# Attention followed by spectral mixing on one core: four weight products moved into the attention loop, the fill work spread evenly, and three first sums placed in PSUM ahead of z

## The chip, the core and the metric

The kernel runs on one core of a Trainium2 chip. The core has TensorE (PE, matrix products into the PSUM memory), VectorE (DVE), ScalarE (ACT), GpSimd (POOL) and SyncE (SP). Each engine executes its own instructions in order, and semaphores tie the engines to one another. Sixteen DMA engines move data; here POOL issues the loads of weights and inputs, and SP issues the stores. The metric is the device time of one execution in microseconds (us); less is better.

## What is computed

```python
phi(x) = [exp(x@w_phi - m), exp(-(x@w_phi) - m)]      # m = max |x@w_phi| of the row
x = num / den          # q_p (k_p^T v) / (q_p sum k_p), 8 batches x 8 heads x 576 x 64
X = rfft(x, axis=1)    # x as 8 x 576 x 512; the first 64 modes are kept
Yr = Xr@w_r - Xi@w_i   # w_r, w_i: 64 modes x 512 x 512, float32
Yi = Xr@w_i + Xi@w_r
y = irfft(Y, n=576)
u = x + y
out = u + relu(u @ w_ch)
```

The weights `w_r` and `w_i` are 134 MB of the 164 MB that the core reads. They go through the DMA engines once and are turned into bf16 on the way. The kernel never forms `u`: it keeps `x` and `x @ w_ch`, and adds the inverse transform of the modes `y` to the first and of `z = y @ w_ch` to the second.

## The kernel before

**Attention loop** (lines 503 to 572). Sixteen units `(g, bp)` (four groups of 128 channels by four pairs of batches) run through a software pipeline, `n` from -2 to 16. In step `n` the loop handles four units at once: `P` (unit n-1: forward transform, `freq` and `keep_x`), `Q` (unit n: attention), `K` (n+1) and `R` (n+2). `keep_x` writes the modes of unit P into `XTb[g % 2]`, so groups 0 and 2 share a buffer, and 1 and 3. Step 16 has only `P`.

**Weight products.** There are 64 of them; each takes one 1 MB block (8 modes x 128 channels, real or imaginary part). I number them 0 to 63 in the order of `order`. Products 0 to 15 belong to group 0, 16 to 31 to group 1, 32 to 43 to group 2, 44 to 55 to group 3; the last eight are groups 2 and 3 of modes 48 to 63. `mix` issues eight matmuls of 32 rows each. The odd product of a pair completes a block `o` of eight modes. `some(n)` in the loop issues the next `n` products, and `next_w(1)` after each asks POOL for the next weight block that has no buffer yet; a block's buffer is free once its product is done. PE executes a product in its place in the program, so a product whose weights have not landed holds up everything behind it on PE. `X` (line 505) sets how many products a step carries: 8 in step 4, 3 in each later one, none in step 16. 40 products are issued in the loop and 24 after it.

**After the loop** (lines 573 to 973). One `while` loop takes the remaining products from `mixq`. `left` is how many are still to come after the one just issued. Between the products it works off `todo`, a list of 76 items, `fill(n)` at a time:

- `turn` of the first of 36 chunks (128 tokens x 512 channels), and 36 `hold(i)`: each turns the next chunk with PE transposes, multiplies chunk `i` by `w_ch` (four matmuls) and copies the result to `xw`. For the last three chunks the result stays in PSUM instead. The first nine `hold` also carry the steps of `inverse_tables()`, which are mostly DVE work. In all 37 items.
- 39 absorb items: `only_x` and `only_w` for the last three chunks (six items), `all` for the other 33. An absorb adds the inverse transform of the modes in `yall` to the chunk's `x` (`keep_x`, DVE) and that of `zall` to its `xw` (`keep_w`, ACT). These need blocks 0 to 5, the eight chunks of batches 0 and 1 that come last need block 6 too.

With group 3 the odd product completes a block: `yst` (DVE), four transposes, `yT`, the product with `w_ch` and `zst` follow, and `put` sends `yst` and `zst` to `yall` and `zall` by DMA. Block 5 is complete with product 55 (`left` = 8), block 6 with 59, block 7 with 63. The pace of `fill` is set by lines 925 to 929.

**PSUM** has two pools in this part: `pst`, four single banks (tile `pt`, function `bank`), and `pst2`, two pairs of banks (tile `pp`, function `banks`). An absorb with an even number takes a pair and one with an odd number two single banks. The tile framework makes an instruction wait for a free buffer and orders accesses of different engines to one tile.

**The last stage** (lines 908 to 999). `seq` lists 20 outputs (`Last`): two single chunks `(0,0)` and `(0,1)`, then pairs of chunks, two of them of "ninth rows" (`n == 8`), and two single chunks at the end. For each, `base(1)` and `base(0)` put `xw` and `x` into PSUM (q and p), `straight` or `late` add the last blocks' modes (`zst`/`yst`, or `yl`), `relu` takes q through ACT into `rl`, and `store` adds p on DVE and sends the result off. Outputs whose p needs no `base(0)` (the stored chunks and ninth rows, `later`) have `x` added by POOL instead. `ahead` says whose q is made while an output's p is made. `seq[0].base(1)`, `seq[0].base(0)` stand before product 63, `seq[1].base(1)` right behind it.

Of the kernel before, what the change touches and what calls it, by code (L numbers as in the profile page):

```python
# [10 lines left out]
F32 = mybir.dt.float32  # L11
# [8 lines left out]
DMODEL = 512  # L20
# [23 lines left out]
def kernel(  # L44
# [14 lines left out]
    pe, dve, act = (InOrder(tc, e) for e in (nc.tensor, nc.vector, nc.scalar))  # L59
# [297 lines left out]
    mixq = []  # L357
# [45 lines left out]
    def sc(i):  # L403
# [4 lines left out]
        out=ang[:, :, 1, :],  # L408
        in0=sf.unsqueeze(2).to_broadcast([128, 5, 64]),
        in1=mf.unsqueeze(1).to_broadcast([128, 5, 64]),  # L410
# [5 lines left out]
        out=rnd, in0=ang, scalar1=1.0 / S_, scalar2=MAGIC, op0=ALU.mult, op1=ALU.add)  # L416
# [71 lines left out]
    def some(n):  # L488
        for _ in range(n):
            if mixq:  # L490
                key = mixq.pop(0)
                mix(*key, wts.pop(key), XTb[key[0] % 2], lambda: one([128, DMODEL]))
                if key not in held:
                    next_w(1)
# [7 lines left out]

    for n in range(-2, len(units) + 1):
        P, Q, K, R = (unit(n + i) for i in (-1, 0, 1, 2))
        X = 0 if n < 4 or not Q else 6 if n == 4 else 3
        if Q:
            Q.exp_q(0)
        if K:
            K.rows_k(0)
            K.exp_k(0)  # L510
        if Q:
            Q.weigh_v2()
            if unit(n + 2):
                unit(n + 2).load_v()
        if P:
            P.freq()
            P.keep_x()
            if P.bp == NP - 1:
                mixq += [key for key in order if key[0] == P.g and (P.g < 2 or key[1] < 12)]
        if Q:  # L520
            Q.cols_q(1)
            Q.exp_q(1)
        some(1 if X else 0)
        if K:
            K.rows_k(1)
            K.exp_k(1)
        if Q:
            Q.kv()
        some(2 if n == 4 else 0)
        if K:  # L530
            K.rows_q(0)
            K.rows_k(2)
            K.rows_q(2)
            K.rows_q(1)
        if Q:
            Q.cols_q(2)
            Q.keep_kv()
            Q.exp_q(2)
        if K:
            K.exp_k(2)  # L540
            K.weigh_v()
        some(1 if X else 0)
        if R:
            R.turn_k(0)
        if K:
            K.shift_q()
        if R:
            R.turn_k(1)
        if Q:
            Q.num(0)  # L550
        if K:
            K.cols_q(0)
        if R and unit(n + 4):
            unit(n + 4).load_k()
        if Q:
            Q.num(6)
        if R:
            R.turn_q(0)
            R.turn_q(1)
            if unit(n + 4):  # L560
                unit(n + 4).load_q()
        if Q:
            Q.num(12)
        some(X - 2)
        if n == -1:
            forward_table()
        if n < 3:
            next_w((2, 3, 2, 3, 2)[n + 2])
        elif n == 3:
            next_w(1)  # L570
        if n == 6:
            pool.dma_start(wchb, moe_w_ch.rearrange("(dc p) e -> p dc e", p=128))
# [8 lines left out]
    def bank(shape=(128, DMODEL), dt=F32):  # L581
        return pst.tile(list(shape), dt, name="pt", tag="pt")

    def banks(dt=F32):
        return pst2.tile([128, 2, DMODEL * (1 if dt == F32 else 2)], dt, name="pp", tag="pp")
# [238 lines left out]
    class Last:  # L824
# [8 lines left out]
        def base(self, which):  # L833
            if self.first:
                if which:
                    self.pp = banks()
                    self.q, self.p = [self.pp[:, 1]], [self.pp[:, 0]]
            elif which:
                self.q = [bank() for _ in self.items]
            else:  # L840
                self.pp = banks()
                self.p = [self.pp[:, a] for a in range(2)]
            for a, (bp, n) in enumerate(self.items):
                turned = ident_b if self.later else perm
                if self.later and not which:
                    continue
                if which:
                    pe.matmul(self.q[a], lhsT=turned, rhs=xw[:, bp, n, :],
                              start=True, stop=False)
                else:  # L850
                    pe.matmul(self.p[a].rearrange("p (g e) -> p g e", g=4), lhsT=turned,
                              rhs=chunk(bp, n), start=True, stop=False)
# [6 lines left out]
                back((self.q if which else self.p)[a], n, bp, CL, yl,  # L859
                     slice(r, r + 32), True, self.later and not which)  # L860

        def straight(self, which):
            if self.early:
                for a, (bp, n) in enumerate(self.items):
                    pe.matmul((self.q if which else self.p)[a], lhsT=CM[n // 4][:, n % 4],
                              rhs=(yst, zst)[which], start=False, stop=True)

        def keep_p(self):
            self.rl = pb.tile([128, 2, DMODEL], F32, name="rl")
            act.copy(self.rl[:, 0], self.p[0])  # L870

        def relu(self):
            if self.later:
# [10 lines left out]
        def store(self):  # L884
            (bp, n), w = self.items[0], len(self.items)
            if w == 1:
                o = pw.tile([128, DMODEL], F32, name="ofr", tag="wt")
            else:
                o = pw.tile([128, 2, DMODEL], F32, name="of", tag="wt")
            if self.first:  # L890
                dve.scalar_tensor_tensor(out=o, in0=self.q[0], scalar=0.0, in1=self.rl[:, 0],
                                         op0=ALU.max, op1=ALU.add)
            elif w == 1:
                dve.tensor_tensor(out=o, in0=self.p[0], in1=self.rl[:, 0], op=ALU.add)
            else:
                dve.tensor_tensor(out=o, in0=self.pp, in1=self.rl, op=ALU.add)
            if n == 8:
                sp.dma_start(
                    bass.AP(tensor=out.tensor, offset=out.offset + (2 * bp * S_ + 8) * DMODEL,
                            ap=[[9 * DMODEL, 128], [2 * S_ * DMODEL, 2], [1, DMODEL]]), o)  # L900
                return
            rows = out[2 * bp + n // 4]
            sp.dma_start(
                bass.AP(tensor=rows.tensor, offset=rows.offset + n % 4 * DMODEL,
                        ap=[[9 * DMODEL, 64], [4 * DMODEL, 2], [1, w * DMODEL]]),
                o.rearrange("p a e -> p (a e)") if w > 1 else o)

    pairs = [[((bp, n), (bp, n + 1)) for n in (0, 2, 4, 6)] for bp in range(NP)]
    seq = [Last((0, 0)), Last((0, 1))] + [Last(*x) for x in pairs[0][1:] + pairs[1] + pairs[2][:3]]
    seq += [Last(*pairs[3][0]), Last((0, 8), (1, 8)), Last(*pairs[3][1]), Last((2, 8), (3, 8))]  # L910
    seq += [Last(*x) for x in (pairs[3][2], pairs[2][3])] + [Last((3, 6)), Last((3, 7))]
    H = DMODEL // 2
    while mixq:
        key = mixq.pop(0)
# [2 lines left out]
            next_w(1)  # L917
        if not mixq:
            assert not todo
            seq[0].base(1)  # L920
            seq[0].base(0)
        mix(*key, wts.pop(key), XTb[g % 2], bank)
        next_w(1)
        left = len(mixq)
        if left > 8:
            h = max(len(todo) - A - 1, 0)
            n = min(h, max(1, math.ceil(h - 2.5 * (left - 9))))
        else:
            n = 4 if left == 8 else math.ceil(len(todo) / (left - 0.2)) if left else 0
        if g == NG - 1 and i == 1:  # L930
            end = left == 0
            if end:
                seq[1].base(1)
            py = pys.pop(o)
            yst = pb.tile([128, DMODEL], BF16, name="yst")
            pt = [bank([128, 2, 128], BF16) for h in range(2)]
# [15 lines left out]
            if o < 5:  # L952
                fill(min(n - 1, 1))
            elif end:
                seq[0].straight(0)
                seq[0].keep_p()
                seq[1].base(0)
            cut = (slice(0, 384), slice(384, DMODEL))
            pz = [bank([128, e.stop - e.start]) for e in cut]
            for e in range(2):  # L960
# [10 lines left out]
        else:  # L971
            fill(n)
    assert not todo
    seq[1].straight(0)
    seq[1].keep_p()
    seq[2].base(1)
    for i in range(3):
        seq[i].straight(1)
    seq[2].relu()
    seq[0].store()  # L980
    seq[1].store()
    ahead = [3, 4, 5, 6, 7, 8, 11, 10, 13, 12, 15, 14, 17, 16, 18, 19]
    for g in range(2, len(seq)):
        s, ts = seq[g], [seq[i] for i in ahead[g - 2:g - 1]]
        for t in ts:
            t.base(1)
            t.straight(1)
        s.base(0)
        s.straight(0)
        for t in ts:  # L990
            t.late(1)
        s.late(0)
        for t in ts:
            t.relu()
        s.store()
        if g == 5:
            seq[9].base(1)
            seq[9].late(1)
            seq[9].relu()
    pb_cm.__exit__(None, None, None)  # L1000
    pw_cm.__exit__(None, None, None)

# [28 lines left out]
```

## Time and profile before

| | us |
|---|---|
| median of 5 runs (range) | 442.43 (442.23 to 443.61) |
| the profiled execution | 442.3 |
| its span, first to last instruction | 440.5 |
| PE, DVE, ACT busy | 330.4, 296.3, 279.3 |
| software DMA queue (loads), share of 16 engines | 99.2% |
| mean granted TensorE clock | 0.916 of full speed |
| product 63 starts | 404.31 |
| last output's DVE instruction starts | 433.94 |

The span leaves out 1.8 us around the first and last instruction. The page divides the span into 40 slices of 11 us; the DMA engines are busy in nine tenths or more of every slice from the second to the thirty-sixth. Times below are counted from the start of the span. In a row of a timeline the columns are start, duration, engine, line, operation, output<-inputs, shape and number of instructions; brackets give the idle time ahead of it on its engine, and what ended it. Every instruction shows line 37, because a helper records them all, so rows are told apart by the names of their tiles.

### The profile page before, as it was taken

The numbers are of one execution on the slowest core, as the hardware profiler recorded it, in microseconds if no ns is written. First come the engines' busy times: TensorE is split into PE (matmuls) and PEld (weight loads), VectorE is DVE, ScalarE is ACT, GpSimd is POOL, SyncE is SP. The second block draws the span as 40 slices with busy tenths as digits, with TensorE's granted clock in tenths as the row PEclk, the third lists the DMA queues.
The fourth block names the chain that finished last, engine by engine and source line by source line (L and its number), as shares of the span: only waits on it lengthen the run. The fifth ranks groups of instructions, "written<-read, shape, count | busy, mean of one in ns | idle before, by whom it ended". The sixth has DMA issues, their size and how long they took to land.

```text
span 440.5 us, 10109 instructions
## 1 busy us (share of the span) xinstructions
PE 330.4 (75%) x4190; PEld 200.1 (45%) x4233; DVE 296.3 (67%) x583; ACT 279.3 (63%) x478; POOL 112.7 (26%) x151
## 2 busy tenths in 40 slices
PE   1676668787778587786787676947887787999992
PEld 0445546555455355464455454623443343333320
DVE  5568787567785775977976776767732233686694
ACT  2787887687897675877876774424443332566781
POOL 6132132132211223221222120211101110483171
PEclk9989988689998896999998896898999989799997
DMA  8999999999999999999999999999999999995797
GB/s 193 210 210 210 236 214 237 232 218 243 232 211 239 224 228 232 237 214 234 229 219 238 212 238 230 221 213 212 212 225 221 219 219 219 212 219 129 242 364 293
DMA packets 51711, 99.55 MB, mean 226 GB/s; under 512 B 2513, under 2 KB 13649, under 8 KB 51665
## 3 DMA queue, kind: packets, MB, share of 16 engines
q0 software_dynamic: 45232, 85.86, 99.2%
q1 hardware_dynamic: 6432, 13.04, 8.5%
q8 instruction: 33, 0.54, 0.5%
q14 instruction: 14, 0.11, 0.1%
HBM read 163.64 MB, written 9.44 MB: 393 GB/s over the span
## 4 chain that ended last, share of the span: by engine, by line
DMA 42%; PE 29%; DVE 14%; ACT 10%; issue 4%; POOL 0%; ACTq 0%; DVEq 0%; POOLq 0%; SPq 0%
DMA vn<-in_v_dram 18%; DMA wt<-in_moe_w_i_dram 16%; PE pt L37 11%; PE one L37 8%; DMA kb<-in_k_dram 5%; PE two L37 5%; PE pp L37 4%; ACT AB L37 4%; DVE mk L37 3%; DVE m L37 3%; DMA qb<-in_q_dram 2%; DVE xs L37 2%; DMA zall<-zst 2%; DVE va L37 1%; ACT xw L37 1%
## 5 line engine op out<-in xcount | busy, mean ns | idle before, releaser
L37 ACT ACTIVATE AB<-two 128x1024 bf16<-128x1024 f32 x64 | 62.0, 1026 | 15.2 <-DVE mk L37 12.8
L37 ACT ACTIVATE AQ<-two 128x1024 bf16<-128x1024 f32 x64 | 62.6, 1045 | 3.5 <-PE two L37 3.4
L37 ACT CAST xw<-pt 128x512 bf16<-128x512 f32 x50 | 29.4, 588 | 45.3 <-PE pt L37 45.1
L37 DVE TENSOR_REDUCE m<-two 128x8 f32<-128x1024 f32 x32 | 39.2, 1224 | 16.2 <-PE two L37 16.1
L37 DVE TENSOR_REDUCE mk<-two 128x8 f32<-128x1024 f32 x32 | 38.9, 1219 | 9.3 <-PE two L37 9.3
L37 DVE TENSOR_TENSOR va<-vn,ee 128x1152 bf16<-128x1152 f32 x32 | 42.0, 1357 | 4.3 <-DMA vn<-in_v_dram 4.2
L37 POOL DMA_DIRECT2D wt<-in_moe_w_i_dram x28 | 21.0, 749 | 87.3 <-PE pt L37 33.9
L37 POOL DMA_DIRECT2D wt<-in_moe_w_r_dram x30 | 22.5, 749 | 69.4 <-PE one L37 29.0
L37 PE MATMUL pt<-wchb,xT 128*128 128x512 bf16 x126 | 36.3, 399 | 4.5 <-DVE xT L37 3.3
L37 PEld LDWEIGHTS <-xs 128*128 128x128 bf16 x624 | 31.5, 103 | 12.3 <-issue 7.8
L37 PE MATMUL two<-w2blk,qT 128*128 128x256 bf16 x128 | 22.3, 303 | 17.7 <-ACT AB L37 9.2
L37 ACT COPY qT<-one 128x512 bf16<-128x512 bf16 (+1 forms) x32 | 19.3, 641 | 25.0 <-PE one L37 24.8
L37 PEld LDWEIGHTS <-XT 128*32 128x32 bf16 x512 | 14.8, 149 | 35.7 <-issue 22.6
L37 PEld LDWEIGHTS <-qT 128*128 128x128 bf16 x144 | 14.6, 104 | 35.5 <-issue 31.9
L37 PE MATMUL two<-mT,minus 96*128 96x512 bf16 x64 | 26.8, 419 | 3.1 <-issue 1.1
L37 PE MATMUL one<-kvz,AQ 128*128 128x65 bf16 x512 | 27.1, 207 | 1.5 <-ACT qT L37 1.1
L37 PEld LDWEIGHTS <-AQ 128*128 128x128 bf16 x512 | 24.4, 107 | 8.0 <-issue 4.4
L37 PE MATMUL one<-wt,XT 128*32 128x512 bf16 x272 | 24.7, 449 | 4.3 <-DVE XT L37 2.7
L37 DVE TENSOR_TENSOR xs<-one,rd 128x384 bf16<-128x384 f32 x48 | 26.8, 558 | 1.6
L37 PE MATMUL two<-w2blk,kT 128*128 128x256 bf16 x128 | 21.2, 295 | 8.0 <-ACT AB L37 8.0
L37 DVE RECIPROCAL rd<-one 128x6 f32<-128x6 f32 x48 | 9.4, 196 | 26.0 <-PE one L37 26.0
L37 PE MATMUL pt<-wt,XT 128*32 128x512 bf16 x192 | 16.5, 418 | 13.2 <-DMA wt<-in_moe_w_i_dram 10.2
(149 smaller groups left out, 720.6 us busy)
## 6 DMA issues: line engine op xcount, KB each, us to landing
wt<-in_moe_w_r_dram POOLq DMA_DIRECT2D x30, 1024.0 KB, 28.6
wt<-in_moe_w_i_dram POOLq DMA_DIRECT2D x28, 1024.0 KB, 28.9
out_dram<-of SPq DMA_DIRECT2D x16, 512.0 KB, 4.6
vn<-in_v_dram POOLq DMA_DIRECT2D x14, 576.0 KB, 25.0
kb<-in_k_dram POOLq DMA_DIRECT2D x16, 288.0 KB, 21.6
qb<-in_q_dram POOLq DMA_DIRECT2D x16, 288.0 KB, 20.5
xs<-in_moe_w_i_dram POOLq DMA_DIRECT2D x2, 1024.0 KB, 24.2
vn<-in_v_dram SPq DMA_DIRECT2D x2, 576.0 KB, 6.4
```

What stands on the lines that cost most here:

```text
L37: ins = f(*args, **kwargs)
```

## The change

It has three parts.

1. In the attention loop, step 12 issues one product more (product 31, the last of group 1, which stood behind the `keep_x` of step 13 that writes the buffer it reads) and step 16 issues three (products 41 to 43), so 44 products stand in the loop and 20 after it. An assertion states that no product of group g-2 is still waiting when `keep_x` overwrites its buffer.
2. The pace: three `fill` items follow each of the first ten of the 20 products, two the eleventh, then 2 at `left` = 8 and 7, 7, 7, 7, 6, 6, 2 after. Before it was 1, 1, 1, 3, 2, 3, 2, 3, 2, 3, 2, 3, 2, 3, 2, then 4 at `left` = 8 and 6, 6, 6, 6, 6, 5, 4.
3. The last stage: q of the two single chunks shares one pair of banks, p of each has a single bank, and both results share one `rl` buffer. Before product 63 now stand `base(1)` of the first two outputs, `base(0)` of the first and `base(0)` of the third, which takes the other pair. The third output's p gets its first half of `yst` ahead of z. `base(0)` and `straight(0)` of the second output stand behind z. The third and fourth outputs are written out by hand ahead of the loop; the ninth rows and the stored pairs of batches 4 and 5 come later in `seq`.

```diff
-        X = 0 if n < 4 or not Q else 6 if n == 4 else 3
+        X = 0 if n < 4 else 6 if n == 4 else 3
...
+            assert not any(key[0] == P.g - 2 for key in mixq)
             P.keep_x()
...
-        some(X - 2)
+        some(X - 2 + (n == 12))
...
             if self.first:
                 if which:
-                    self.pp = banks()
-                    self.q, self.p = [self.pp[:, 1]], [self.pp[:, 0]]
+                    if not two_q:
+                        two_q.append(banks())
+                    self.q = [two_q[0][:, self.items[0][1]]]
+                else:
+                    self.p = [bank()]
...
-        def straight(self, which):
+        def straight(self, which, only=(0, 1)):
...
         def keep_p(self):
-            self.rl = pb.tile([128, 2, DMODEL], F32, name="rl")
-            act.copy(self.rl[:, 0], self.p[0])
+            if not two_p:
+                two_p.append(pb.tile([128, 2, DMODEL], F32, name="rl"))
+            self.rl = two_p[0][:, self.items[0][1]]
+            act.copy(self.rl, self.p[0])
...
-    seq = [Last((0, 0)), Last((0, 1))] + [Last(*x) for x in pairs[0][1:] + pairs[1] + pairs[2][:3]]
-    seq += [Last(*pairs[3][0]), Last((0, 8), (1, 8)), Last(*pairs[3][1]), Last((2, 8), (3, 8))]
-    seq += [Last(*x) for x in (pairs[3][2], pairs[2][3])] + [Last((3, 6)), Last((3, 7))]
+    two_q, two_p = [], []
+    seq = [Last((0, 0)), Last((0, 1))] + [Last(*x) for x in pairs[0][1:] + pairs[1]]
+    seq += [Last(*x) for x in (pairs[2][1], pairs[2][0], pairs[3][0], pairs[2][2], pairs[3][1])]
+    seq += [Last((0, 8), (1, 8)), Last(*pairs[3][2]), Last((2, 8), (3, 8)), Last(*pairs[2][3])]
+    seq += [Last((3, 6)), Last((3, 7))]
...
-            seq[0].base(1)
-            seq[0].base(0)
+            for c in seq[:2]:
+                c.base(1)
+            for c in (seq[0], seq[2]):
+                c.base(0)
         mix(*key, wts.pop(key), XTb[g % 2], bank)
...
-            h = max(len(todo) - A - 1, 0)
-            n = min(h, max(1, math.ceil(h - 2.5 * (left - 9))))
+            n = -(-max(len(todo) - A - 2, 0) // (left - 8))
+        elif left == 8:
+            n = 2
         else:
-            n = 4 if left == 8 else math.ceil(len(todo) / (left - 0.2)) if left else 0
+            n = math.ceil(len(todo) / max(left - 0.6, 0.4)) if left else 0
...
-            if end:
-                seq[1].base(1)
...
                 seq[0].straight(0)
                 seq[0].keep_p()
-                seq[1].base(0)
+                seq[2].straight(0, (0,))
...
     assert not todo
+    seq[1].base(0)
     seq[1].straight(0)
     seq[1].keep_p()
+    for i in range(2):
+        seq[i].straight(1)
+    seq[2].straight(0, (1,))
     seq[2].base(1)
-    for i in range(3):
-        seq[i].straight(1)
+    seq[2].straight(1)
     seq[2].relu()
     seq[0].store()
     seq[1].store()
-    ahead = [3, 4, 5, 6, 7, 8, 11, 10, 13, 12, 15, 14, 17, 16, 18, 19]
-    for g in range(2, len(seq)):
+    seq[3].base(1)
+    seq[3].straight(1)
+    seq[2].store()
+    seq[3].base(0)
+    seq[3].straight(0)
+    seq[3].relu()
+    ahead = [4, 5, 6, 7, 8, 9, 12, 11, 14, 13, 16, 15, 17, 18, 19]
+    for g in range(3, len(seq)):
...
-        s.base(0)
-        s.straight(0)
+        if g > 4:
+            s.base(0)
...
-        if g == 5:
-            seq[9].base(1)
-            seq[9].late(1)
-            seq[9].relu()
+        if g == 7:
+            seq[10].base(1)
+            seq[10].late(1)
+            seq[10].relu()
```

## The prediction

> **What bounds the kernel now.** I read the page's rows on DMA first, then the table of stretches, then PE's timeline around the places that change, and at last the waits of the last stage. The loads' queue is busy 99.2% of the span, and the stretches below show a DMA share over 1 until 404: with the weights queued in order, product 63 cannot run before its block lands. That block is issued at 370.09 and lands 33.7 us later (the row of its issue), at 403.79; the product starts at 404.31. So two things meet at 404: the weights, and the work that must be finished by then.
>
> ```profile
> core 0: us, PE busy (x) PEld busy (x) DVE busy (x) ACT busy (x) POOL busy (x), PEclk, DMA share, GB/s
> 286.40:303.10 16.70, 9.09 (x80) 4.83 (x77) 11.36 (x54) 4.72 (x9) 2.23 (x3) 0.90 1.12 212
> 303.10:362.00 58.90, 48.06 (x380) 25.33 (x389) 25.79 (x71) 24.69 (x46) 7.42 (x10) 0.97 1.12 218
> 362.00:372.40 10.40, 7.85 (x59) 3.75 (x59) 4.40 (x10) 1.61 (x4) 1.48 (x2) 1.00 1.12 223
> 372.40:404.30 31.90, 30.21 (x156) 10.81 (x157) 22.09 (x37) 20.01 (x37) 18.31 (x18) 0.89 1.02 204
> 404.30:434.70 30.40, 28.01 (x160) 9.35 (x160) 23.22 (x25) 20.75 (x39) 11.39 (x10) 1.00 0.78 290
> ```
>
> The reader is to see that PE has air only before 372 and little after. PE's timeline says where:
>
> ```profile
> 288.34 0.66 PE L37 MATMUL pt<-wt,XT 128*32 128x512 bf16 x8 [0.88 <-DMA wt<-in_moe_w_i_dram]
> 293.26 0.66 PE L37 MATMUL pt<-wt,XT 128*32 128x512 bf16 x8 [2.84 <-DMA wt<-in_moe_w_r_dram]
> 298.21 0.86 PE L37 MATMUL pt<-wt,XT 128*32 128x512 bf16 x8 [2.88 <-DMA wt<-in_moe_w_i_dram]
> ...
> 351.89 0.66 PE L37 MATMUL pt<-wt,XT 128*32 128x512 bf16 x8 [2.29 <-DMA wt<-in_moe_w_i_dram]
> ...
> 362.02 0.66 PE L37 MATMUL pt<-wt,XT 128*32 128x512 bf16 x8 [0.47 <-DMA wt<-in_moe_w_i_dram]
> ...
> 372.47 0.38 PE L37 MATMUL pp<-zall,CI 96*128 96x512 bf16 x1 [0.87 <-DMA zall<-zst]
> ```
>
> These are products 41, 42, 43, 53, 55 and the first use of block 5's z. Counting the products between them too, PE waits for weights 13.1 us from 286.5 to 362.0 (0.88 + 2.84 + 2.88 + 0.83 + 2.87 + 2.29 + 0.47). After 372.5 no product waits for its weights any more: the 33 full absorbs run back to back and end just when block 63 lands. That is the balance the change disturbs.
>
> **Part 1, four products moved.** Each product issues on PE for 0.6 us and frees a buffer for one POOL load. Product 31 in step 12 costs PE 0.6 us there, and a wait of 2.74 us for `keep_x` (the product at 246.63) goes; both end ahead of 286, where products wait for weights anyway. Its load (block 40) now stands ahead of the last v load on POOL's queue, which may land v some 5 us later (a block's spacing at 283 to 303). The last unit's v is already waited for (0.53 us at 277.8), so the loop may end 5 us later, at about 291.5. That is hidden too: products 42 and 43 stand in step 16 behind their weights, which land at 293.2 and 298.2. DMA never starves, so block 63 still lands at 403.8.
>
> What is not hidden: step 16 now holds PE until product 43 at 298.2, and product 44, the first of the `while` loop, until 303.14 (issue at 271.34 plus 31.8). Only then does the first `turn` go. Before, three `todo` items were done by 295.3 and three more by 306.9.
>
> **Part 2, the pace.** From 286.47 to 362.02 are 75.55 us, less 13.06 of waits: 62.5 us of work for 15 products, 33 items and five blocks. After the change the same stretch starts at 303.14 with 11 products and 32 items to do: 62.5 - 4 x 0.6 - 1.1 (an item past the tables, from the 2.9 us of a product with two of them at 346.65) = 59.0 us. To that comes the table work which ran under the waits at 288 to 298: DVE's small operations there last from 291.3 to 294.8, and little else could run; I take 3 us of it. So product 55 starts at about 303.1 + 62 = 365.1, against 362.0: **3 us late**. Bounds: 1.5 (all hidden, fewer clock dips) and 5. Three items per product are even, but little is left to catch up with: two products with six items and one block take 2.9 + 1.1 + 5.4 (329.96 to 335.40) = 9.4 us, two weight blocks 10.7 (58.8 from 303.14 to 361.96, over eleven).
>
> Behind product 55 the chain is fixed: 3.5 us to the sending of z (362.02 to 365.51) and 6.8 to its landing. So z of block 5 is there at 375.4 in place of 372.33. The five `hold` items that are left (2 + 3; before 4) fill this wait in part, and product 57, ready at 373.2, fits in too, where before it stood behind all six short absorbs. The first full absorb then starts at about 376.8 against 375.5: **1.3 us late**. From there PE, DVE and ACT have the same work in another order, 0.6 us of DVE per absorb (0.69 busy, overlapping), so the last absorb is 1.3 us late as well. The pace itself (7, 7, 7, 7, 6, 6, 2) gains nothing, because the absorbs were not waiting for products.
>
> **A rule on the clock.** After stretches in which PE was mostly idle this trace shows half the clock, though not after all:
>
> ```profile
> 289.80:293.20 3.40, 0.62 (x6) 0.31 (x4) 3.13 (x24) 1.07 (x2) 0.00 (x0) 1.00 1.12 213
> 293.20:296.60 3.40, 2.08 (x20) 1.18 (x21) 2.11 (x14) 1.07 (x2) 0.74 (x1) 1.00 1.12 212
> ...
> 349.70:353.10 3.40, 1.20 (x13) 0.64 (x14) 0.51 (x2) 0.52 (x1) 0.24 (x1) 1.00 1.12 224
> 353.10:356.50 3.40, 3.36 (x14) 1.74 (x14) 1.30 (x4) 0.86 (x2) 0.50 (x1) 0.51 1.12 212
> ```
>
> The Trainium skill ("TensorE: Matmul & The Clock Gate", section "What's actually happening") says that PE falls to half its clock after an idle window of about 3.4 us and comes back after as long a busy one. It speaks against the change: in step 16 PE would do 0.6 us of work in every 5. By the rule the new stretch begins at half clock (up to 1.7 us lost); in return the dip at 353 goes, since no wait is left (1.7 gained). By the rows, a wait of 2.3 us is followed by half clock once and one of 2.8 us not at once. Both give about nothing net; I add nothing, and keep 2 us either way in the range, because the absorbs now have no slack against a dip: the one at 373.6 to 380.5 stretched a matmul from 0.38 to 0.63 us.
>
> **Part 3, before product 63.** `base(0)` of the third output needs the second pair of banks. The last absorb (number 32 from 0, even, so a pair) holds it until ACT has copied it:
>
> ```profile
> 404.31 0.66 PE L37 MATMUL pt<-wt,XT 128*32 128x512 bf16 x8
> 404.46 0.59 ACT L37 CAST xw<-pp 128x512 bf16<-128x512 f32 x1 [0.23 <-DVE xs L37]
> ...
> 405.10 0.10 PEld L37 LDWEIGHTS <-CF 128*128 128x128 bf16 x1 [0.57 <-ACT xw L37]
> ```
>
> Before, `seq[1].base(1)` waits for this pair at 405.10, but product 63 stands ahead of it. Now the two matmuls of `base(0)` stand ahead of product 63: 405.10 + 2 x 0.22 = 405.5, so even on-time absorbs push product 63 from 404.3 to 405.5 (+1.2). With the 1.3 us from part 2 it starts at **406.8**, 2.5 us late. Queued behind it on PE are its own eight matmuls, and behind them `yst`, z and every output.
>
> **Part 3, after it.** From `zst` on PE has 7 matmuls to the third output instead of 8, q of the second output no longer waits for ACT's copy of its p, and `relu` of the third output does not wait for the first store, as both share one `rl`. The third output's DVE instruction, 3.1 us behind `zst` (407.9 to 411.0), comes about 0.7 us sooner by these, the fourth and fifth about 1 us. But then the extra output (`seq[10]` at `g == 7`, before `seq[9]` at `g == 5`) takes the two banks that the ninth's q needs, and DVE has its gap there instead (1.05 us ahead of 418.00). From that point DVE has one output per 1.2 us in both kernels; I count no gain at DVE's end, bounds -0.5 and +0.3. The stores gain something: from 421.8 on they take 4.3 to 5.0 us to land, before that 3.0, so a queue has built up. With more sent early and the rest later it is shorter: -0.5, bounds 0 and -1.
>
> **Sum.** 1.3 + 1.2 + 0 - 0.5 = +2.0 us on the profiled execution's 442.3, which stands 0.1 under the median: **444.3 us**.
>
> **Rivals.**
> *The weights stay the bound* (faster). If the fill work keeps up with 3 items per product (block 5 not over 0.5 us late) and no half clock falls on the absorbs, they end by 402.5, product 63 goes at 403.85 (-0.45) and the shorter queue of stores adds -0.5 to -1: 441.2. For it: PE is busy for only 48.1 of 58.9 us from 303 to 362. Against: that air was the waits, and 16 us at the front are given up.
> *A wash* (within 0.2%, which is 0.9 us, about what a measurement of this kernel can tell from no change). The absorbs end 0.7 us early because product 57 uses the wait for z, which half pays for the bank: 442.5. For it: PE idles 2.4 us between 369.7 and 373.5. Against: block 5 must then be on time.
> *Half clock on the absorbs* (slower, more). One mechanism: an idle stretch while z of block 5 is awaited, then two windows at half clock, and again after. It costs 2 us more per 6.8 us of it: 446.3. It decides once the absorbs end behind 403.
> *The first part alone does nothing*: product 31 only fills a gap; then parts 2 and 3 stay as computed.
>
> **Chances.** Forecast 0.5, half clock 0.17, wash 0.14, weights 0.19. The first two are slower, with a little lost to the wash: slower 0.66, same 0.15, faster 0.19. The range reaches from the weights' case, 441.3, to just over the half clock's, 447.0; the forecast's own range is 443.2 to 446.
>
> **What would show it.** Right: product 44 near 303.2 with no `todo` item before it; products 46 to 55 without waits for weights, 55 near 365; z of block 5 landing near 375; ahead of product 63 two `base(0)` matmuls that wait for ACT's last `xw<-pp`; the product near 406.8; the third output's DVE instruction about 2.4 us behind `zst`. Wrong: weights waited for at products 48 to 55, or product 63 within 0.2 us of the landing of its block.

## The result, and the profile after

The changed kernel takes 441.04 us in the median of 43 runs (440.23 to 443.10) against 442.20 us in 80 runs of the kernel before; the ratio is 0.9974, with a 95% interval of 0.9967 to 0.9982. It is **faster by 0.26%**, some 1.2 us, where 444.3 and slower was forecast. The profiled execution took 440.13 us, its span 438.4 us.

The same stretches as were shown of before, from the table of stretches of the changed kernel:

```profile
core 0: us, PE busy (x) PEld busy (x) DVE busy (x) ACT busy (x) POOL busy (x), PEclk, DMA share, GB/s
286.40:303.10 16.70, 8.79 (x128) 5.43 (x125) 5.04 (x12) 2.07 (x6) 3.59 (x5) 0.70 1.12 212
303.10:362.00 58.90, 51.58 (x400) 27.54 (x408) 33.95 (x117) 26.99 (x49) 6.89 (x10) 0.93 1.12 218
362.00:372.40 10.40, 9.53 (x73) 4.66 (x73) 3.37 (x9) 3.20 (x6) 1.54 (x3) 1.00 1.12 223
372.40:404.30 31.90, 29.04 (x172) 10.96 (x172) 24.85 (x42) 20.66 (x38) 18.31 (x18) 1.00 1.01 200
404.30:434.70 30.40, 26.40 (x148) 8.90 (x147) 22.50 (x23) 20.16 (x38) 11.37 (x10) 0.99 0.84 311
```

Table work and `hold` items have moved from the first stretch to the second, as the pace says (DVE 11.36 to 5.04 us, then 25.79 to 33.95). The line that matters is the fourth: the stretch of the full absorbs now has the full clock, 1.00 for 0.89. Over the whole span the granted clock did not rise but fell, from 0.916 to 0.906: half clock has moved to the first two stretches (0.70 for 0.90, 0.93 for 0.97), where part of it lies under waits for weights. In the last stretch, DMA moves 311 GB/s for 290.

PE's timeline of the changed kernel, at products 43, 44 and 55, the first use of block 5's z with product 57 behind it, and product 63 with the third output's `base(0)` ahead of it:

```profile
296.98 0.66 PE L37 MATMUL one<-wt,XT 128*32 128x512 bf16 x8 [3.56 <-DMA wt<-in_moe_w_i_dram]
301.99 1.07 PE L37 MATMUL pt<-wt,XT 128*32 128x512 bf16 x8 [4.35 <-DMA wt<-in_moe_w_r_dram]
...
363.21 0.66 PE L37 MATMUL pt<-wt,XT 128*32 128x512 bf16 x8
...
373.49 0.39 PE L37 MATMUL pp<-zall,CI 96*128 96x512 bf16 x1
373.81 0.66 PE L37 MATMUL pt<-wt,XT 128*32 128x512 bf16 x8
...
402.45 0.59 PE L37 MATMUL pp<-xs,CF 128*128 128x512 bf16 x2 [0.75 <-ACT xw L37]
402.97 0.66 PE L37 MATMUL pt<-wt,XT 128*32 128x512 bf16 x8
```

Behind 302 no product waits for weights: 46 to 54 run up to 10.4 us behind the landing of their blocks, and 55 still 2.7 us behind. The wait for the bank, which the forecast put ahead of product 63, is there (0.75 us), and costs nothing, since block 63 lands at 402.92. In this profile that is close, for the two matmuls behind the wait take until 402.9; in e6, with the same code up to there, PE then still waits 0.79 us for block 63.

When a block lands differs from run to run: the first weight block is issued at 4.47 us in the kernel before and after alike, yet block 63 lands between 402.9 and 405.8 us in the ten profiles of this study (why is not shown). So the kernels are compared by times counted from a landing (us, one profiled execution each; a landing is known to 0.1 us):

| | before | after |
|---|---|---|
| product 55 behind block 55's landing | 0.06 | 2.69 |
| first use of block 5's z behind that landing | 10.5 | 13.0 |
| first full absorb to the end of the last absorb on PE | 28.18 | 25.85 |
| product 63 behind block 63's landing | 0.52 | 0.05 |
| product 63 to the end of the last DVE instruction | 30.32 | 30.66 |
| product 63 to the landing of the last store | 34.95 | 34.09 |

The fourth row gives 0.47 us and the last 0.86 us: 1.33 us, for 1.16 us between the medians. Such differences are not exact: from the landing of block 55 to that of block 63 pass 41.8 us before and 42.4 us after, and 41.2 to 42.4 us over the ten profiles.

The first two rows and the start of the absorbs depend on the execution as well. Four of the runs below (e1, e4, e5, e6) have the loop and the pace of the changed kernel up to product 55; there product 55 is only 0.5 to 1.2 us behind its block, and the first full absorb starts 12.5 to 13.2 us behind the landing of block 55. After has 14.7 us, and the five profiles with the old loop and pace have 13.2 to 14.5 (before 13.5).

**Two questions**: why the absorbs, which in this profile start as late as was forecast, end early; and why the stores land earlier although DVE ends later.

### The profile page after: what moved, and what is told of

The parts are those of the page before. It is cut to its first block, busy times and chain, and to the rows that moved or that the text cites. A ratio compares the mean times of both kernels' runs of the same rounds, so it can differ in the third digit from the quotient of the medians.

```text
span 438.4 us, 10106 instructions
## 1 busy us (share of the span) xinstructions
PE 329.4 (75%) x4190; PEld 201.4 (46%) x4233; DVE 296.3 (68%) x583; ACT 279.4 (64%) x478; POOL 112.8 (26%) x151
## 4 chain that ended last, share of the span: by engine, by line
PE 40%; DVE 20%; ACT 17%; DMA 16%; issue 5%; POOL 0%; POOLq 0%; ACTq 0%; DVEq 0%
PE pt L37 16%; PE one L37 13%; DMA wt<-in_moe_w_r_dram 8%; ACT AB L37 7%; PE two L37 7%; DMA wt<-in_moe_w_i_dram 6%; DVE m L37 5%; DVE mk L37 5%; PE pp L37 4%; ACT AQ L37 3%; ACT XT L37 2%; DVE xs L37 2%; DMA qb<-in_q_dram 2%; DVE XT L37 1%; ACT qT L37 1%
## 5 line engine op out<-in xcount | busy, mean ns | idle before, releaser
L37 ACT ACTIVATE AB<-two 128x1024 bf16<-128x1024 f32 x64 | 62.0, 1026 | 11.5 <-DVE mk L37 8.9
L37 PE MATMUL pt<-wchb,xT 128*128 128x512 bf16 x127 | 35.4, 392 | 5.5 <-DVE xT L37 4.0
L37 ACT COPY qT<-one 128x512 bf16<-128x512 bf16 (+1 forms) x32 | 19.3, 641 | 28.1 <-PE one L37 27.8
L37 PEld LDWEIGHTS <-qT 128*128 128x128 bf16 x144 | 14.7, 104 | 36.6 <-issue 32.7
L37 PE MATMUL one<-wt,XT 128*32 128x512 bf16 x304 | 27.3, 450 | 5.1 <-DMA wt<-in_moe_w_i_dram 3.6
L37 PE MATMUL one<-va,AB 64*128 64x65 bf16 x1024 | 22.7, 199 | 9.1 <-DVE va L37 9.1
L37 DVE COPY xT<-pt 128x512 bf16<-128x512 bf16 x36 | 17.0, 472 | 17.8 <-PE pt L37 17.8
L37 POOL DMA_DIRECT2D kb<-in_k_dram x16 | 11.5, 720 | 62.1 <-PE one L37 53.6
L37 PEld LDWEIGHTS <-XT 128*32 128x32 bf16 x512 | 14.5, 149 | 27.9 <-issue 21.4
## 6 DMA issues: line engine op xcount, KB each, us to landing
wt<-in_moe_w_r_dram POOLq DMA_DIRECT2D x30, 1024.0 KB, 27.8
```

Of the source, the lines that this page charges most:

```text
L37: ins = f(*args, **kwargs)
```

## The experiments

Theory: the wait for block 5's z left PE so idle that its clock fell to half in the first absorbs of the kernel before; the changed pace fills the wait with `hold` items and product 57, the clock stays up, and the slack this gives pays for part 3's wait for the bank, so that part 3's gain in the stores is left over. Rivals: the even pace itself shortens the absorbs; or part 3 alone makes the gain. For the stores, two things of part 3 compete: the first four outputs, and the order of the later ones.

| run | ratio to before (95%) | product 63 behind its block | absorbs | product 63 to last DVE end / last landing |
|---|---|---|---|---|
| e1 | 0.9987 (0.9968 to 1.0007) | 0.06 | 25.84 | 30.32 / 34.95 |
| e2 | 1.0006 (0.9987 to 1.0026) | 1.41 | 27.99 | 30.98 / 34.11 |
| e3 | 0.9987 (0.9964 to 1.0010) | 0.08 | 26.70 | 30.38 / 34.89 |
| e4 | 0.9974 (0.9957 to 0.9991) | 1.12 | 27.83 | 31.09 / 34.01 |
| e5 | 0.9975 (0.9953 to 0.9996) | 0.06 | 26.31 | 30.66 / 34.08 |
| e6 | one time, 442.48 us | 0.07 | 26.62 | 29.82 / 34.28 |
| e7 | one time, 442.97 us | 1.15 | 27.20 | 31.58 / 34.61 |
| e8 | 0.9988 (0.9970 to 1.0005) | 0.02 | 26.08 | 30.31 / 34.44 |

The kernel before had medians of 443.48 us beside e1 to e4 and 443.51 beside e5 to e8. The intervals are wide against effects of 0.1 to 0.3%, so the verdicts below rest on the profiles, one execution of each kernel.

**e1_loop_and_pace** and **e2_last_stage** split the change: the kernel before with parts 1 and 2 alone, and with part 3 alone.

```diff
# e1: lines 505, 564 and the pace at 925 to 929 alone
+        X = 0 if n < 4 else 6 if n == 4 else 3
+        some(X - 2 + (n == 12))
+            n = -(-max(len(todo) - A - 2, 0) // (left - 8))
# e2: everything behind line 830 but the pace
+            for c in (seq[0], seq[2]):
+                c.base(0)
```

> Parts 1 and 2 alone (products moved, new pace), the last stage as before. Theory (the clock): z of block 5 lands about 13 us behind the landing of block 55 (as after), the wait for it is filled, there is no half-clock window from 365 to 404, the absorbs take about 25.9 us in place of 28.2 and product 63 starts within 0.2 us of the landing of its block (0.5 before). From product 63 to the last store's landing about 35.0 us, as before. Ratio to before about 0.999. Rival (the stores do it all): product 63 still 0.5 us behind its block, ratio 1.000. Rival (the forecast's backlog): product 63 1 us or more behind its block, ratio over 1.002.

> Part 3 alone (the last stage), loop and pace as before. If the absorbs end as late as before, the two matmuls of base(0) wait for the second pair and product 63 starts 1.2 to 1.7 us behind the landing of its block; from product 63 to the last landing about 34.1 us as after. Ratio 1.000 to 1.001. If the half-clock windows do not fall on the absorbs in this run, product 63 is on time and the ratio is 0.998. Rival (the bank wait costs nothing): product 63 at most 0.5 us behind its block with half clock in the absorbs too, ratio 0.998.

e1 has no half clock from 365 to 404, as the theory said; but z is used only 11.5 us behind the landing of block 55, not 13. The pace alone ends the absorbs 3.1 us ahead of block 63's landing (401.96 and 405.04), where the kernel before had 0.1 us; but product 63 can only start with its weights, so all but 0.46 us of that lies idle. Part 3 alone pays 0.9 us more ahead of product 63 and gets 0.84 back in the stores: nothing. Added, the two give -0.4 us; together they give -1.33, because the wait for the bank falls into the slack. In the profiles, neither part alone makes the gain. The timed runs point the same way (0.9987 and 1.0006 apart, 0.9974 together) but cannot show it, as e1's interval reaches beyond 0.9974. The clock, in the table of stretches of the kernel before:

```profile
370.00:373.40 3.40, 1.38 (x5) 0.47 (x6) 1.89 (x3) 0.52 (x1) 0.74 (x1) 1.00 1.13 219
373.40:376.80 3.40, 3.28 (x15) 0.80 (x15) 0.21 (x1) 1.23 (x3) 0.00 (x0) 0.54 1.12 213
376.80:380.20 3.40, 3.40 (x10) 1.20 (x9) 2.37 (x4) 1.89 (x4) 1.24 (x2) 0.50 1.12 211
```

the same of e2, with the old pace:

```profile
370.00:373.40 3.40, 1.22 (x6) 0.34 (x4) 1.89 (x3) 0.58 (x1) 0.51 (x1) 0.96 1.14 217
373.40:376.80 3.40, 3.40 (x15) 0.92 (x15) 0.35 (x1) 1.16 (x2) 0.00 (x0) 0.50 1.13 216
376.80:380.20 3.40, 3.40 (x10) 1.16 (x8) 2.22 (x4) 2.03 (x4) 1.38 (x2) 0.53 1.11 208
```

and of the changed kernel:

```profile
370.00:373.40 3.40, 2.83 (x17) 1.31 (x15) 1.42 (x3) 0.00 (x0) 0.07 (x1) 1.00 1.13 227
373.40:376.80 3.40, 3.32 (x22) 1.28 (x21) 1.85 (x4) 1.89 (x4) 0.00 (x0) 1.00 1.14 215
376.80:380.20 3.40, 3.32 (x22) 0.99 (x21) 2.88 (x6) 3.09 (x6) 2.89 (x3) 1.00 1.11 208
```

With PE busy for 1.2 to 1.4 us in the 3.4 us of the wait, two windows at half clock follow; with 2.83 us, none. From 376.8 to 380.2 the changed kernel has 22 matmuls where the others have 10.

**e3_two_holds_later** and **e4_no_holds_left** change one number each, the items issued at `left` = 8: fewer in the kernel before, and more in the changed one, so that its wait for z has no `hold` left to fill it.

```diff
# e3, to the kernel before
-            n = 4 if left == 8 else math.ceil(len(todo) / (left - 0.2)) if left else 0
+            n = 2 if left == 8 else math.ceil(len(todo) / (left - 0.2)) if left else 0
# e4, to the changed kernel
         elif left == 8:
-            n = 2
+            n = 5
```

> Before, with one number changed: 2 items instead of 4 at left = 8, so that two more hold items stand behind product 56, in the wait for z. Theory (the clock): the wait is partly filled, no half clock from 365 to 404, absorbs about 26 us, product 63 within 0.2 us of its block; ratio about 0.999. Rival (the clock dips by chance): half clock in the absorbs about as often as before; the absorb stretch 28 us, ratio 1.000.

> After, with 5 instead of 2 items at left = 8, so that all hold items stand ahead of product 56 and nothing fills the wait for z. Theory (the clock): PE idles about 2 to 3 us before z lands, one or two windows of half clock follow, the absorbs take 28 us or more, the second pair is free late and product 63 starts 1 to 3 us behind its block; ratio to before 1.001 to 1.005. Rival (chance): no change against after, ratio 0.997.

In the profiles both go the theory's way: e3 has no half clock in its absorbs (one window at 366.9 us instead, before they begin), and they take 26.7 us; in e4 half clock is back at 377.5 us, they take 27.8 us, and product 63 is 1.12 us late. The rows of e4:

```profile
374.05:377.46 3.41, 2.25 (x16) 0.67 (x15) 1.84 (x4) 1.66 (x3) 0.43 (x1) 1.00 1.12 210
377.46:380.88 3.42, 3.42 (x15) 1.02 (x8) 1.76 (x3) 1.17 (x2) 1.15 (x1) 0.50 1.12 212
```

e4's timed runs miss their expectation: 0.9974, no slower than the changed kernel. Its profiled execution (443.47 us) is the slowest of its twelve, so half clock need not have fallen on the absorbs in each of them; no view shows it for the others. So that the clock in the absorbs moves the median is not shown: the evidence for it is in the profiles.

**e8_before_kept_busy** adds nothing useful at all: the kernel before, with the PE sums of the three `only_x` items, which stand in the wait for z, formed four times over.

```diff
# in the function behind the only_x items
-            self.sum_p(bank())
+            p = bank()
+            for _ in range(4):
+                self.sum_p(p)
```

> Before, with each of the three only_x sums formed four times over (the same sum each time, so the result is the same): nine more matmuls of PE work, or some 2 us, in the wait for z of block 5, nothing else moved. Theory (the clock): no half-clock window from 366 to 404, the absorbs take 25.9 to 26.5 us instead of 28.2, product 63 starts within 0.2 us of its block (0.5 before); ratio 0.999. Rival (order, not clock: the absorbs got shorter because the hold items and product 57 were placed otherwise): the absorbs still take 28 us or, with the clock full, the stretch is still over 27; product 63 0.5 us behind.

Its table of stretches:

```profile
363.20:366.60 3.40, 2.96 (x17) 1.80 (x18) 1.12 (x4) 0.85 (x2) 0.74 (x1) 0.56 1.12 211
...
373.40:376.80 3.40, 2.73 (x22) 0.87 (x19) 1.25 (x2) 1.66 (x3) 0.00 (x0) 1.00 1.12 211
376.80:380.20 3.40, 3.32 (x19) 1.21 (x20) 3.11 (x6) 2.15 (x4) 1.69 (x2) 1.00 1.13 213
```

The old pace, the old last stage and more work for PE, and yet the absorbs are 2.1 us shorter and product 63 starts 0.02 us behind its block. So the pace is not what shortens them: PE's clock is, and the work in the wait holds it up. One window at half clock is left at 363.6, ahead of the absorbs.

The ten profiles agree. Where the wait for z has no work added (before, e2, e7, e4), half clock falls on the absorbs, and they take 27.2 to 28.2 us; where it has (after, e1, e3, e5, e6, e8), none does, and they take 25.8 to 26.7. The absorbs as one stretch each, before, e2, e7, e4 and after:

```profile
375.51:403.69 28.18, 27.33 (x146) 10.24 (x144) 21.50 (x36) 17.73 (x34) 18.31 (x18) 0.91 1.03 206
375.37:403.36 27.99, 27.14 (x146) 10.16 (x144) 21.49 (x36) 17.72 (x34) 18.29 (x18) 0.92 1.07 210
377.44:404.64 27.20, 26.33 (x147) 9.86 (x144) 21.40 (x36) 17.67 (x34) 18.34 (x18) 0.95 1.02 203
376.61:404.44 27.83, 26.90 (x153) 10.14 (x153) 21.84 (x36) 19.43 (x36) 18.23 (x18) 0.94 1.04 205
375.20:401.05 25.85, 24.92 (x145) 9.63 (x145) 21.65 (x36) 19.26 (x36) 18.31 (x18) 1.00 1.08 212
```

Length times granted clock gives 25.6, 25.8, 25.8, 26.2 and 25.9 us: but for the clock the absorbs are equally long to within 0.6 us, whatever the pace. The longest at full clock (e3, e5, e6: 26.3 to 26.7) hold a wait for weights of 0.4 to 0.5 us. e7 also bears on e8: the old pace too, with nothing added in the wait, it has half clock from 376.6 to 380.0 and product 63 1.15 us behind its block.

**e5_third_base_behind** takes the wait for the bank out of product 63's way in the changed kernel.

```diff
-            for c in (seq[0], seq[2]):
-                c.base(0)
+            seq[0].base(0)
...
             if end:
+                seq[2].base(0)
```

> After, with base(0) of the third output moved from ahead of product 63 to right behind it, into the time in which PE waits for yst (0.5 us idle). Theory: with the absorbs on time this costs nothing and product 63 no longer depends on ACT's last copy, so it starts within 0.1 us of its block's landing whatever the clock does; from product 63 to the last landing 34.1 us as in after (at most 0.3 more). Ratio to before 0.997. If base(0) there delays yst's transposes, the last stage is 0.4 us longer and the ratio 0.998.

Nothing changes: 0.06 us behind its block for 0.05, and 34.08 us to the last landing for 34.09. With the absorbs at full clock the wait is free; in e2, with late absorbs, it was not.

**e6_after_old_order** and **e7_before_new_order** exchange the order of the later outputs (`seq`, `ahead`, and where the extra output is made), and leave the first ones as they were.

```diff
# e6, to the changed kernel; e7 does the reverse to the kernel before
-        if g == 7:
-            seq[10].base(1)
+        if g == 5:
+            seq[9].base(1)
```

> After, with the old order of outputs (ninth rows and stored pairs as before, their extra output at g == 5). From product 63 to the last landing: 34.95 us before, 34.09 after. Theory (the first stores matter): the third output's DVE instruction stays 6.2 us behind product 63 (6.7 before), stores land 4.4 us or less behind their issue, total 34.1 to 34.4. Rival (the order of the outputs matters): stores at the end land 4.6 to 5.0 us behind their issue, total 34.8 to 35.0.

> Before, with the new order of outputs alone. Theory (the first stores matter): from product 63 to the last landing 34.7 to 35.0 us, as before (34.95), landings at the end 4.5 us or more behind the issue. Rival (the order of the outputs matters): 34.1 to 34.4, landings 4.0 us.

Most of the gain seems to be in the first outputs: with them alone (e6) 34.28 us, with the order alone (e7) 34.61, with both 34.09, with neither 34.95. e6 meets the theory's total, its landings (4.5 us) just miss it; e7 meets neither, with a total between theory and rival and landings of 3.5 us. But e8 and e3 have the old last stage too, with 34.44 and 34.89 us, so such a number is good to about half a microsecond, and how the gain is shared between the two stays open. All four with neither (before, e1, e3, e8) lie from 34.44 to 34.95, all four with both (after, e2, e4, e5) from 34.01 to 34.11.

What does stand out is that DVE's end and the end of the kernel go their own ways. e6 ends DVE 0.84 us sooner than the changed kernel and lands 0.19 us later; e7 ends it 1.26 us later than the kernel before and lands 0.34 us sooner. The stores show a part of why. DMA issues from 403 us on, of the kernel before (size, and median us from issue to landing):

```profile
out_dram<-of SPq DMA_DIRECT2D x16, 512.0 KB, 4.6
```

of the changed kernel:

```profile
out_dram<-of SPq DMA_DIRECT2D x16, 512.0 KB, 4.0
```

of e6:

```profile
out_dram<-of SPq DMA_DIRECT2D x16, 512.0 KB, 4.5
```

and of e7:

```profile
out_dram<-of SPq DMA_DIRECT2D x16, 512.0 KB, 3.5
```

This median does not settle it alone: e8, with the last stage of the kernel before, has 3.8.

And the table of stretches from 4 us behind product 63, 8 us each; the kernel before:

```profile
408.31:416.31 8.00, 7.88 (x38) 3.05 (x38) 5.55 (x6) 4.99 (x11) 0.00 (x0) 1.00 0.73 224
416.31:424.31 8.00, 8.00 (x50) 2.38 (x49) 6.54 (x6) 6.94 (x14) 5.35 (x5) 1.00 0.83 333
424.31:432.31 8.00, 7.24 (x45) 1.94 (x42) 7.61 (x8) 5.89 (x12) 6.03 (x6) 1.00 0.99 393
```

and the changed kernel:

```profile
406.97:414.97 8.00, 8.00 (x43) 3.10 (x42) 5.94 (x6) 5.49 (x11) 0.00 (x0) 1.00 0.83 269
414.97:422.97 8.00, 7.89 (x50) 2.27 (x46) 6.31 (x7) 6.82 (x14) 4.49 (x4) 1.00 0.76 304
422.97:430.97 8.00, 7.26 (x44) 2.10 (x42) 7.11 (x7) 6.00 (x12) 6.88 (x7) 1.00 1.00 398
```

From 20 us behind product 63 DMA is full in both (share 0.99 and 1.00, 393 and 398 GB/s), and an output of 512 KB takes 524288 B / 395 GB/s = 1.33 us there, longer than DVE's 1.23. DVE then runs ahead into a queue. What then counts is how many bytes have gone before: the changed kernel moves 269 GB/s for 224 in the first 8 us (0.36 MB more), loses 0.23 MB of that in the next 8, where DVE waits 1.23 us for PE ahead of 418.92, and is some 0.13 MB ahead, by this estimate 0.3 us. That explains a part of the 0.86 us; the rest comes about as the last stores drain, and is not explained.

## Why the prediction was wrong, step by step

- **Product 44, the weights, product 55**: right. 44 starts at 301.99 with no item of `todo` ahead of it, nothing waits for weights behind it, and 55 is 2.69 us behind its landing (forecast 3). In absolute time it is 363.2 and not 365.1, for its block came 1.45 us earlier in this execution. That the 3 us came out is partly luck: e1, e4, e5 and e6 have 0.5 to 1.2 us, under the forecast's lower bound of 1.5. The backlog is at most 8.9 to 10.4 us in these five profiles and falls by about 1.3 us with every two products, as the prediction's own 9.4 us of work against 10.7 of weights says; its sum for product 55 did not use that.
- **z of block 5**: right. It is used 13.0 us behind the landing of block 55 (forecast 13.4), and the first full absorb starts 12.0 us behind product 55 (forecast 11.7). In e1, e4, e5 and e6, z is used 10.8 to 11.5 us behind the landing.
- **"so the last absorb is 1.3 us late as well"**: this is the step that failed, together with the clock's **"Both give about nothing net; I add nothing"**. The last absorb ended 1.2 us sooner behind the landing of block 55 than before (40.5 for 41.7 us), and 1.9 us ahead of block 63. The sum took the absorbs' 28.2 us over as if they were work. They were about 25.8 us of work, and the rest was half clock; the dip at 373.6 to 380.5 stood in the prediction as a danger for the changed kernel, and only the rival of the weights let it go. The sum did not read it as a loss of the kernel before which the filled wait could end. The rule from the Trainium skill ("TensorE: Matmul & The Clock Gate", section "What's actually happening") was weighed at step 16 and at 353 us, and not at the one wait in front of the stretch that sets the end. The prediction had seen that the five `hold` items and product 57 fall into that wait, and took only the start of the absorbs from it.
- **The wait for the bank, +1.2**: right as a mechanism, and with late absorbs in size too (e2: 1.41 us behind the landing, 0.9 more than before). With the absorbs 1.9 us ahead of the landing it is free (0.05 us behind the landing with the wait, 0.06 without it in e5). The prediction's own sign of being wrong, product 63 within 0.2 us of its block, came true. The error of the step above cost 1.3 + 1.2 us, and hid the 0.5 that could be gained ahead of product 63.
- **DVE's end 0, stores -0.5**: DVE's end came 0.34 us later and the stores gained 1.20, both just outside their bounds; the sum is -0.86. The two terms were added as if each counted; but DVE's end can move by 0.8 us without the last landing following (e6), as the queue of stores stands between. Of the 0.86 us, 0.3 are accounted for.
- **The rival that came true** is the weights as the bound (441.2 us: -0.45 ahead of product 63, -0.5 to -1 behind; measured -0.47 and -0.86). Of its two conditions, no half clock on the absorbs was met; block 5 no more than 0.5 us late was not met and not needed. The range ended at 441.3 and missed 441.04 us by a quarter of a microsecond.

Not tried: the extra output at a later `g`, where a queue of stores would cover DVE's wait of 1.23 us. None of the versions run beats the changed kernel by its profile or its ratio; e4 and e5 equal its ratio.

## What to carry to other kernels

Before a stretch in which PE sets the pace is carried over into a sum, multiply its length by its granted clock: what is over is no work, and a change that only fills the wait in front of it can take it away. Two changes that each give little can give something together, when one makes slack at a meeting point and the other has a wait to hide there. Where the stores at the end keep the DMA engines full, count the bytes that have gone by then, and not only the end of the engine that makes them.

## What the hardware showed unexpectedly

PE need not stand still for its clock to fall. In all ten traces the granted clock is either full or half, and changes only on a grid of steps of 3.41 us, which lies elsewhere in each execution. The kernel before, cut on its grid at two places:

```profile
288.31:291.72 3.41, 2.03 (x19) 1.04 (x19) 3.29 (x18) 1.07 (x2) 0.74 (x1) 1.00 1.13 213
291.72:295.13 3.41, 1.87 (x20) 1.02 (x20) 3.03 (x24) 0.00 (x0) 0.74 (x1) 1.00 1.12 213
295.13:298.55 3.42, 0.55 (x12) 0.37 (x9) 0.35 (x1) 1.07 (x2) 0.00 (x0) 1.00 1.12 213
298.55:301.96 3.41, 3.41 (x24) 1.80 (x16) 2.71 (x9) 0.61 (x2) 0.74 (x1) 0.50 1.12 212
...
370.23:373.64 3.41, 1.30 (x6) 0.34 (x4) 1.89 (x3) 0.59 (x1) 0.60 (x1) 1.00 1.12 216
373.64:377.05 3.41, 3.41 (x15) 0.93 (x15) 0.46 (x1) 1.16 (x2) 0.00 (x0) 0.50 1.13 213
```

Steps with 2.03 and 1.87 us of PE work were followed by full clock, steps with 0.55 and 1.30 us by half. Over the ten traces, of the steps at full clock, all 84 with less than 1.4 us of PE work were followed by half clock, 59 of 94 with 1.4 to 1.8 us, five of 110 with 1.8 to 2.3 us, and none of 684 with more. This also explains why a stretch cut elsewhere can mislead: the 0.62 us from 289.8 to 293.2 is spread over two steps with enough work in each. In the wait for z, the step ahead of the absorbs holds 1.30 us (before), 1.36 (e2), 2.17 (e7) and 2.25 (e4), with half clock behind it, and 2.17 (e3), 2.74 (e8) and 2.83 or more (after, e1, e5, e6), with none. So e3, with as much work there as e7, stands on the edge; the other five have more.
